# Moving the loads of two x tiles from SyncE's queue to ScalarE's at the start of a linear-attention block

## The chip, the cores and the metric

The kernel runs on one core of one Trainium2 chip. The metric is the device time of one execution in microseconds (us), smaller is better; the median of several runs counts. A profile is one further execution, recorded by the hardware profiler.

## What is computed

A block over one sequence of 2048 tokens with width 640: a layer norm without weights, then two branches from the normalized x, multiplied and added to the input.

```python
xn = (x - mean) / sqrt(var + 1e-5)                 # x: [2048, 640]
q, k, v = split_heads(xn @ wqkv)                   # 32 heads of 20
pq, pk = phi(q), phi(k)                            # t + 1 for t > 0, else exp(t); + 1e-6
kv = einsum("hsd,hse->hde", pk, v);  z = pk.sum(s)
s = ((pq @ kv) / (pq @ z + 1e-6)) @ wo             # linear attention, not causal
g = silu(relu(xn @ w1) @ w2)                       # w1: [640, 1728], w2: [1728, 640]
out = x + s * g
```

Inputs, weights and output are bfloat16.

## The kernel before

The tokens are 16 tiles of 128 (`T`), four tiles to a chunk of 512 columns. The work has a head, in which the first tiles are normalized, and a long body in which TensorE multiplies with few gaps.

**Normalizing.** Tiles 0 to 3 go a short way. ScalarE takes the sum of a tile (`ma`, L685, `mean_act`), or of its second half where VectorE's `bn_stats` (`ba`, `mh`, L637 and L679) takes the first. VectorE subtracts the mean (`ce`, L695 and L699, `centre`), TensorE transposes the centred tile with an identity matrix (`tr`, L706) and VectorE (`cd`) or ScalarE (`ca`) copies the transposed tile out of PSUM (L716, L718). Tiles 4 to 7 have `bn_stats` for mean and variance (`S`). All tiles are then normalized by VectorE (`N`, L673, `LN_norm`; it overwrites the centred tile, so it waits until TensorE has read that), and each `N` ends with a DMA transpose on SyncE's queue (L722, `xnT_dma`), which writes the transposed tile that the body multiplies with. The first eight of these transposes are those of tiles 0 to 7, in the order 1, 4, 5, 7, 6, 0, 2, 3.

**Key products.** `k012` is the part of tile 0's key product that uses weight rows 128 to 255 (row blocks 1 to 2); it multiplies on TensorE at L733 (`K_mm`) and needs the centred, transposed tile and the key weights. The key weights come in three loads (L586, `wk_load`): `lk02` with row blocks 0 and 1 (320 KB), `lk24` with 2 and 3 (320 KB), and `lk45` with block 4.

**Body.** Large products are done by a seven-product scheme of the Strassen kind (`unit`): products at L1164 accumulate in PSUM, and VectorE forms the sums of weight blocks, the sums of activations, and some additions from PSUM to PSUM, all through one helper (`tt`, L936). `SQ` forms the sums of the query weights, `wq`, a part of `reg6`; its first sum is written to a part of `pqT`. The query weights come by one load of 800 KB, `lq` (L567).

**Loads.** `lx3` loads x tile 3 on SyncE's queue and `ax1` loads x tile 1 on ScalarE's (L562, `x_load`, 160 KB a tile); `lx8` is a pair of tiles. `lw` loads a piece of w1 (L582).

**What sets the order.** The text `PROGRAM` lists all steps in order. A step becomes one or several recorded operations with the engine, the tiles it reads and writes, and so its dependencies. A planner (`Sched.place`, with the costs of `cost` and of `_record`) simulates the engines with estimated durations. TensorE and SyncE take their operations in the order of the text; in the head (up to the bar `|`) so do all other engines. After the bar ScalarE, VectorE and GpSimd take, among the next 60 recorded operations (`LOOK`), the one that is ready first by the planner's estimate, or a more urgent one. `emit` then writes each engine's instructions in that planned order with waits on semaphores. On the chip the order is fixed: an instruction that waits holds up all that follow it on its engine.

Of the kernel before, what the change touches and what calls it, by code (L numbers as in the profile page):

```python
# [343 lines left out]


PROGRAM = """
lx0 lx2 ax1 ba0 mh0 ma0 lk02 lx3 lk24 ce0 lx4 ma1 ce1 lx5 lk45 lx7 lw2 tr0 pf3 cd0 lx6 bb0 ma2 sq1
ce2 cd1 ma3 tr1 k001 lw5 cd2 k012 ba3 lw3 ca3 mh3 ag0 ce3 S4 tr2 k102 S5 ca4 k023 k123 k134 ca5 k201
lw0 N1 tr3 N4 sq2 k213 S7 ca6 k035 ca7 k145 N5 ke0 k235 S6 bb3 N7 ag3 k301 k312 kr0 ke1 kr1 F1
N6 k325 ke2 P4 N0 kr2 P11 P5 F0 ke3 P10 KT5 kr3 KT4 N2 N3 |  # L350
# [1631 lines left out]
```

## Time and profile before

| | |
|---|---|
| median of 3 runs | 202.5 us (201.94 to 203.0) |
| profiled execution: its own time | 202.56 us |
| its span (first to last instruction) | 201.3 us |
| granted TensorE clock | 1.00 |
| busy share of the span: TensorE, VectorE, ScalarE, GpSimd | 98%, 86%, 66%, 19% |
| DMA | 30.43 MB, mean 151 GB/s |

In the rows of the timeline the columns are start and duration in us, the engine, the line of the kernel, the operation, and output and input by tile name with buffer numbers left out (`reg<-reg` can be two different tiles). In brackets stands how long the engine was idle before and what released it. `SPq` and `ACTq` are the DMA issues of SyncE and ScalarE; "DMA to landing" counts from the issue to the last increment of the DMA's semaphore. `x4` is a count of instructions merged into one row. A wait for several semaphores is put down to the one that came last by the profile; where the named engine was long done, another, often a DMA, was the last.

### The profile page before, as it was taken

The page shows a single profiled execution, that of the slowest core. Times are in us where ns is not written, and L with a number is a line of the kernel's source. Part 1 is how long each engine was busy: PE and PEld are TensorE (multiplying, and loading weights), DVE is VectorE, ACT ScalarE, POOL GpSimd, SP SyncE. Part 2 cuts the span into 40 slices and gives each one's busy share as a digit, 9 for nine tenths or more (in the row PEclk, how much of TensorE's full clock was granted, in tenths as well). Part 3 has the DMA queues.
Part 4 walks back from the last instruction along what each step waited for, and adds up shares of the span by engine and source line. Part 5 has one row for each costly group of instructions (what it writes and reads, how often), then busy time and mean ns, then how long its engine had stood idle before and what let it go on. Part 6 is the DMA issues. An engine that isn't in the chain of part 4 may idle for free.

```text
span 201.3 us, 3641 instructions
## 1 busy us (share of the span) xinstructions
PE 197.2 (98%) x1312; PEld 120.1 (60%) x1312; DVE 173.2 (86%) x407; ACT 132.5 (66%) x280; POOL 37.7 (19%) x66
## 2 busy tenths in 40 slices
PE   8899999999999999999999999999999999999995
PEld 2656534554564554545454777777777777777773
DVE  5998799999999989999568998999867699866565
ACT  6798958998999998868832514363545355536533
POOL 3584003143345646422000000000000000000000
PEclk9999999999999999999999999999999999999999
DMA  5999695345466798854304985975952711011113
GB/s 179 335 259 95 150 351 144 70 98 109 108 145 134 150 256 174 171 99 67 113 17 118 270 264 184 295 212 148 355 185 72 258 65 36 33 67 65 36 65 98
DMA packets 38455, 30.43 MB, mean 151 GB/s; under 512 B 13733, under 2 KB 38437, under 8 KB 38437
## 3 DMA queue, kind: packets, MB, share of 16 engines
q1 hardware_dynamic: 32853, 23.62, 41.8%
q0 software_dynamic: 4624, 5.57, 14.3%
q10 hardware_dynamic: 960, 1.02, 1.7%
q8 instruction: 10, 0.16, 0.4%
q14 instruction: 8, 0.07, 0.1%
HBM read 15.81 MB, written 5.24 MB: 105 GB/s over the span
## 4 chain that ended last, share of the span: by engine, by line
PE 90%; DVE 4%; DMA 2%; ACT 1%; issue 1%; DVEq 0%
PE psT L991 43%; PE psT L1164 32%; PE psT L733 6%; PE psT L1494 2%; PE psT L823 2%; DMA reg<-reg 1%; ACT regE L743 1%; PE psT L1838 1%; DMA reg<-in_A_x_dram 1%; PE psT L841 1%; PE psT L1629 1%; PE psT L1603 1%; DVE stats L637 1%; DVE regX L936 1%; PE psT L895 1%
## 5 line engine op out<-in xcount | busy, mean ns | idle before, releaser
L1164 PE MATMUL psT<-reg 128*128 128x512 bf16 (+2 forms) x166 | 45.0, 370 | 0.0
L991 PE MATMUL psT<-reg,regH 128*128 128x320 bf16 (+1 forms) x224 | 35.0, 299 | 0.0
L991 PE MATMUL psT<-reg 128*128 128x320 bf16 (+1 forms) x178 | 28.4, 299 | 0.0
L991 PEld LDWEIGHTS psT<-reg,regH 128*128 128x128 bf16 (+1 forms) x224 | 21.9, 98 | 8.5
L1164 PEld LDWEIGHTS psT<-reg 128*128 128x128 bf16 (+1 forms) x166 | 15.9, 98 | 16.9 <-DVE regH L1217 0.6
L863 POOL DMA_DIRECT2D regH<-reg x16 | 18.6, 1188 | 20.9 <-DMA regH<-reg 9.4
L991 PEld LDWEIGHTS psT<-reg 128*128 128x128 f16 (+1 forms) x178 | 17.3, 98 | 7.4 <-DVE regE L899 0.4
L936 DVE TENSOR_TENSOR reg<-reg 128x1024 f16<-128x1024 bf16 (+11 forms) x30 | 19.0, 646 | 2.2 <-PE psT L991 1.8
L998 ACT ACTIVATE reg<-psT 128x320 f32<-128x320 f32 (+1 forms) x24 | 10.5, 436 | 15.8 <-PE psT L991 14.8
L1214 ACT ACTIVATE regH<-psT 128x512 bf16<-128x512 f32 (+1 forms) x24 | 14.6, 612 | 5.8 <-PE psT L1164 5.3
L1665 ACT ACTIVATE wv_sb<-psT 128x320 bf16<-128x320 f32 (+2 forms) x23 | 9.6, 424 | 11.4 <-PE psT L991 11.0
L991 PE MATMUL psT<-reg,pqT 128*128 128x320 bf16 (+1 forms) x84 | 15.8, 299 | 0.0
L936 DVE TENSOR_TENSOR psT<-psT,reg 128x320 f32<-128x320 f32 (+1 forms) x21 | 11.4, 543 | 2.8 <-PE psT L991 2.8
L637 DVE BATCH_NORM_STATS2 stats<-reg 128x6 f32<-128x320 bf16 x28 | 12.3, 480 | 1.4 <-DMA reg<-in_A_x_dram 1.1
L1853 ACT ACTIVATE reg<-psT 128x640 bf16<-128x640 f32 (+1 forms) x14 | 8.0, 570 | 7.5 <-PE psT L991 7.5
L733 PE MATMUL psT<-reg 128*128 128x320 bf16 x80 | 12.3, 299 | 0.0
L936 DVE TENSOR_TENSOR reg<-psT,reg 128x320 bf16<-128x320 f32 (+1 forms) x16 | 7.8, 489 | 5.1 <-PE psT L991 5.1
L1171 ACT ACTIVATE psT<-psT 128x512 f32<-128x512 f32 (+1 forms) x18 | 10.6, 594 | 1.8 <-PE psT L1164 1.7
L800 ACT ACTIVATE regE<-psT 128x512 bf16<-128x512 f32 x16 | 9.5, 603 | 2.6 <-PE psT L1164 2.5
L998 ACT ACTIVATE psT<-psT 128x320 f32<-128x320 f32 x17 | 7.2, 425 | 5.6 <-PE psT L991 5.5
L936 DVE TENSOR_TENSOR reg<-reg,wv_sb 128x640 bf16<-128x640 bf16 (+1 forms) x15 | 6.8, 456 | 4.3 <-ACT reg L1853 3.5
L733 PEld LDWEIGHTS psT<-reg 128*128 128x128 bf16 x80 | 7.7, 98 | 4.5 <-issue 0.4
(174 smaller groups left out, 400.0 us busy)
## 6 DMA issues: line engine op xcount, KB each, us to landing
regH<-reg POOLq DMA_DIRECT2D x16, 320.0 KB, 3.8
reg<-in_B_w_dram SPq DMA_DIRECT2D x12, 320.0 KB, 4.9
scr<-rden SPq DMA_DIRECT2D x4, 640.0 KB, 7.0
reg<-in_A_x_dram SPq DMA_DIRECT2D x4, 640.0 KB, 6.1
out_dram<-reg SPq DMA_DIRECT2D x14, 160.0 KB, 1.8
regE<-scr SPq DMA_DIRECT2D x3, 640.0 KB, 6.1
reg<-in_A_x_dram SPq DMA_DIRECT2D x4, 320.0 KB, 4.8
reg<-in_A_x_dram SPq DMA_DIRECT2D x7, 160.0 KB, 4.3
```

The lines of the kernel that those rows point to most:

```text
L637: sc.op("DVE", lambda eng: eng.bn_stats(stats[:, t, a, :], xv[:, HN * a:HN * (a + 1)]), R=[("xin", xs(t))], W=[("stats", t, a)])
L733: fns.append(lambda eng, a=a, k=k, lhs=lhs: eng.matmul(ps[bk[a]][:, 0:HN], lhsT=lhs, rhs=wk[:, k, HN * a:HN * (a + 1)], start=(k == 0), st ...
L800: exps.append(sc.op("ACT", lambda eng: eng.activation(out=e_, in_=src, func=ACTF.Exp), R=[key], W=[("er_e", es)]))
L863: dma("POOL", lambda eng: eng.dma_start(zacc[a], src, **kw), R=[key] + after, W=[("zacc", a)], chain=zchain[a])
L936: sc.op("DVE", lambda eng: eng.tensor_tensor(out=out, in0=in0, in1=in1, op=op), R=R, W=W, extra=extra)
L991: sc.group("PE", [(lambda eng, k=k, lhs=lhs, rhs=rhs: eng.matmul(ps[b][:, 0:HN], lhsT=lhs, rhs=rhs, start=(start and k == 0), stop=(k == n ...
L998: sc.op("ACT", lambda eng: eng.activation(out=dst, in_=ps[b][:, 0:HN], func=ACTF.Copy), R=[("ps", b)], W=[dkey], extra=extra)
L1164: sc.group("PE", [(lambda eng, k=k, lhs=lhs, rhs=rhs: eng.matmul(ps[b][:, 0:nn], lhsT=lhs if tile is None else rhs, rhs=rhs if tile is Non ...
L1171: sc.op("ACT", lambda eng: eng.activation(out=dst[:, 0:nn], in_=ps[b][:, 0:nn], func=ACTF.Copy), R=[("ps", b)], W=[dkey], extra=extra)
L1214: sc.op("ACT", lambda eng: eng.activation(out=dst, in_=ps[b], func=ACTF.Relu), R=[("ps", b)], W=[("hT", j, f)], extra=ex)
L1665: sc.op("ACT", lambda eng, lo=lo, hi=hi: eng.activation(out=g[:, lo:hi], in_=src[:, lo - HN * n:hi - HN * n], func=ACTF.Silu), R=[key, ("s ...
L1853: sc.op("ACT", lambda eng: eng.activation(out=o_[:, 0:n].rearrange("p (a n) -> p a n", a=2) if n == D else o_[:, 0:n], in_=src, func=ACTF. ...
```

## The change

One line of `PROGRAM` changes. The loads of x tiles 2 and 3 leave SyncE's queue (`lx2`, `lx3`) and stand behind that of x tile 1 on ScalarE's (`ax2`, `ax3`). SyncE's queue then begins with x tile 0, `lk02`, `lk24` and goes on with x tile 4 as before.

```diff
 PROGRAM = """
-lx0 lx2 ax1 ba0 mh0 ma0 lk02 lx3 lk24 ce0 lx4 ma1 ce1 lx5 lk45 lx7 lw2 tr0 pf3 cd0 lx6 bb0 ma2 sq1
+lx0 ax1 ax2 ax3 ba0 mh0 ma0 lk02 lk24 ce0 lx4 ma1 ce1 lx5 lk45 lx7 lw2 tr0 pf3 cd0 lx6 bb0 ma2 sq1
 ce2 cd1 ma3 tr1 k001 lw5 cd2 k012 ba3 lw3 ca3 mh3 ag0 ce3 S4 tr2 k102 S5 ca4 k023 k123 k134 ca5 k201
```

Both names call the same function; the second only names another engine as issuer:

```python
        "lx": x_load,
        "ax": lambda t: x_load(t, 1, "ACT"),
```

Since the planner simulates the whole kernel, other operations can move in its order too.

## The prediction, made before the result was known

> **What bounds the kernel now.** I read the page's busy table first, then TensorE's own rows and the chain of waits, and last the rows of SyncE, VectorE and ScalarE up to 30 us.
>
> ```profile
> span 201.3 us, 3641 instructions
> PE 197.2 (98%) x1312; PEld 120.1 (60%) x1312; DVE 173.2 (86%) x407; ACT 132.5 (66%) x280; POOL 37.7 (19%) x66
> ```
>
> TensorE is busy for 197.2 of 201.3 us. A change at the start can only pay by closing an idle stretch of TensorE, and only if no later stretch opens by as much. The timeline of TensorE has two places where that is decided:
>
> ```profile
> 6.04 0.70 PE L733 MATMUL psT<-reg,regX 128*128 128x320 bf16 x4 [0.63 <-DVE regX L716]
> ...
> 27.17 1.24 PE L823 MATMUL psT<-reg 128*128 128x512 bf16 x5
> 28.58 0.60 PE L1164 MATMUL psT<-regX,reg 128*128 128x512 f16 x2 [0.17 <-DVE psT L936]
> ```
>
> The first key product starts at 6.04 after 0.63 us of idleness. The row names a copy, but the product also waits for the first key weights (`lk02`). Their own row and its time to landing:
>
> ```profile
> L586 SPq DMA_DIRECT2D reg<-in_A_wqkv_dram x1: 434/434/434, 1.7 to 1.7; - x1
> DMA to landing us min/median/max: 4.2/4.2/4.2
> ```
>
> Issued at 1.7, landed at 5.9: this DMA, not the copy, releases the product. The change goes for these 0.63 us.
>
> The second place is the product at 28.58. The chain of waits does not reach it through TensorE but through transposes and VectorE:
>
> ```profile
> 21.05 2.64 DMA reg<-reg
> ...
> 23.72 0.43 DVE regH L936
> ...
> 27.93 0.61 DVE psT L936
> 28.54 0.05 issue
> 28.58 9.24 PE psT L1164 x42
> ```
>
> From 28.58 on, all the rest of the chain up to the last tile is TensorE back to back. So the end of the kernel moves with 28.58, and 6.04 matters only if it moves 28.58.
>
> What leads there starts on SyncE's queue:
>
> ```profile
> 10.17 12.16 SPq L722 DMA_TRANSPOSE reg<-reg  x8
> ...
> 23.00 0.46 SPq L567 DMA_DIRECT2D reg<-in_A_wqkv_dram  x1
> ...
> 17.07 2.61 SPq L722 DMA_TRANSPOSE reg<-reg  x1
> ...
> 21.05 1.28 SPq L722 DMA_TRANSPOSE reg<-reg  x1
> ```
>
> Eight transposes issue back to back from 10.17 to 22.33 (a usual one 1.28 us, one of them 2.61), the last lands at 21.05 + 2.64 = 23.69, and VectorE starts at 23.72. So 28.58 hangs on when the first transpose issues, and that needs the normalized tile 1 from VectorE (L673, 9.74 to 10.14).
>
> **The change part by part.**
>
> **1. Key weights 0.45 us earlier.** On SyncE `lk02` takes the slot of x tile 2, the second of two issues:
>
> ```profile
> 0.79 0.88 SPq L562 DMA_DIRECT2D reg<-in_A_x_dram  x2
> ...
> L562 SPq DMA_DIRECT2D reg<-in_A_x_dram x2: 399/408/417, 0.8 to 1.3; - x2
> DMA to landing us min/median/max: 2.3/2.5/2.7
> ...
> 0.96 0.39 ACTq L562 DMA_DIRECT2D reg<-in_A_x_dram  x1
> ...
> DMA to landing us min/median/max: 2.6/2.6/2.6
> ```
>
> The two end at 0.79 + 0.88 = 1.67 and the second takes 0.42, so `lk02` is issued at 1.25 instead of 1.7. If it keeps its 4.2 us it lands at 5.45 and the first key product starts up to 0.45 us earlier; if the x tiles on the other queue take their share of the DMA engines it lands as late as before. Either way I cost this at nothing: what hides it is the wait at 28.58, where TensorE would idle that much longer. Were that cover gone, it would be worth 0.45 us at most.
>
> **2. x tiles 2 and 3 on ScalarE's queue.** Before, by the rows just shown, x tile 2 lands at 1.25 + 2.7 = 3.95 and x tile 1 (ScalarE's queue, the last two rows) at 0.96 + 2.6 = 3.56. After, x tile 2 is issued behind x tile 1, at some 0.96 + 0.39 + 0.05 = 1.40, and moves beside `lk02`, not ahead of it. ScalarE's own work isn't held up: its third issue is over by about 2.3, and its first mean needs x tile 0, which lands at 0.79 + 2.3 = 3.1.
>
> ```profile
> core 0: us, PE busy (x) PEld busy (x) DVE busy (x) ACT busy (x) POOL busy (x), PEclk, DMA share, GB/s
> 2.20:3.30 1.10, 1.10 (x4) 0.32 (x3) 0.15 (x1) 0.24 (x2) 0.34 (x1) 1.00 1.00 341
> 3.40:4.40 1.00, 0.86 (x4) 0.16 (x3) 0.93 (x4) 1.00 (x5) 0.00 (x0) 1.00 0.81 223
> ```
>
> The engines are full (share 1.00, 341 GB/s) up to 3.3; then, when the key weights begin, they slow down to 223 GB/s. If x tile 2 shares evenly with `lk02`, 2 x 160 KB must move after x tile 1: 0.96 us at 341 GB/s, 1.47 us at 223. So x tile 2 lands at 4.5 to 5.0. I take 4.75; the ends are 4.0 (no sharing: 1.40 + 2.6) and 5.9 (1.40 plus the 4.5 us of x tile 4, below). The Trainium skill (DMA: Bandwidth & Descriptors, Issuing engines are not separate DMA queues) says that DMAs of several issuing engines interleave on the same 16 DMA engines and that a second queue saves only issue time. By that rule the sum is the one I take below; without sharing it would be that of rival (b).
>
> Who waits for x tile 2? ScalarE's mean, then VectorE's centring, then everything behind it on VectorE in its fixed order:
>
> ```profile
> 4.34 0.72 ACT L685 ACTIVATE regE<-reg 128x640 bf16<-128x640 bf16 x1
> ...
> 6.33 0.47 ACT L685 ACTIVATE regE<-reg 128x320 bf16<-128x320 bf16 x1 [0.46 <-DMA reg<-in_A_x_dram]
> ...
> 5.38 0.37 DVE L695 TENSOR_SCALAR reg<-reg,msum 128x640 bf16<-128x640 bf16 x1
> 5.67 0.55 DVE L716 COPY regX<-psT 128x384 bf16<-128x384 bf16 x2
> 6.34 0.49 DVE L637 BATCH_NORM_STATS2 stats<-reg 128x6 f32<-128x320 bf16 x1
> ...
> 7.12 0.45 DVE L699 TENSOR_SCALAR reg<-reg,msum 128x640 bf16<-128x640 bf16 x1
> 7.70 0.89 DVE L637 BATCH_NORM_STATS2 stats<-reg 128x6 f32<-128x320 bf16 x2
> ...
> 9.74 0.40 DVE L673 TENSOR_SCALAR reg<-reg,msum,rsy 128x640 bf16<-128x640 bf16 x1
> ```
>
> The mean moves from 4.34 to 4.78, 0.44 later, and the centring at 5.38 with it. Two gaps on VectorE take some of it back: 6.22 to 6.34 (waiting for x tile 3, which now comes earlier) and 7.57 to 7.70 (x tile 4, issued at 3.2 and landed 4.5 later, at 7.7):
>
> ```profile
> L562 SPq DMA_DIRECT2D reg<-in_A_x_dram x1: 467/467/467, 3.2 to 3.2; - x1
> DMA to landing us min/median/max: 4.5/4.5/4.5
> ```
>
> x tile 4 has the same bytes ahead of it as before, so it lands no later than 7.7 and does not bind. Tile 1's normalization, and with it the first transpose, comes 0.44 - 0.12 - 0.13 = 0.19, say 0.2 us later. Ends: 0.25 earlier (both gaps closed, x tile 2 in time) and 1.3 later (x tile 2 at 5.9: 1.55 - 0.25).
>
> **3. The planner's new order on VectorE.** The built program differs in one more place. TensorE's order is the same, but on VectorE, by line:
>
> ```
> before: L761, L637, L936 psT<-psT, L936 regX, L936 pqT<-reg6, L637, L936 pqT
> after:  L761, L936 pqT<-reg6, L936 psT<-psT, L936 regX, L936 pqT, L637, L637
> ```
>
> `pqT<-reg6` (first sum of `SQ`) reads the query weights, the load `lq` that SyncE issues behind all eight transposes and `lx8`. It now stands ahead of the addition into PSUM on which TensorE waits at 28.58.
>
> ```profile
> 27.04 0.48 DVE L761 TENSOR_TENSOR reg<-regE 128x640 bf16<-128x640 bf16 x1
> 27.44 0.49 DVE L637 BATCH_NORM_STATS2 stats<-reg 128x6 f32<-128x320 bf16 x1
> 27.84 0.68 DVE L936 TENSOR_TENSOR psT<-psT,wv_sb 128x512 f32<-128x512 f32 x1
> ...
> 28.76 0.42 DVE L936 TENSOR_TENSOR pqT<-reg 128x512 f16<-128x512 bf16 x1
> 29.10 0.49 DVE L637 BATCH_NORM_STATS2 stats<-reg 128x6 f32<-128x320 bf16 x1
> ...
> reg<-in_A_wqkv_dram SPq DMA_DIRECT2D x1, 800.0 KB, 5.3
> ```
>
> `lq` lands at 23.00 + 5.3 = 28.3. VectorE would be ready for the sum at 27.44, waits 0.86 us, spends 0.34 on it (28.76 to 29.10) and starts the addition at 28.66 instead of 27.84: 0.82 us later. Queued behind the waiting instruction are that addition and all later VectorE work; TensorE waits for the addition. Transposes, VectorE's chain and `lq` all shift with the first transpose, so 0.82 and the 0.2 of part 2 add up. Ends: a gain of 0.06 if `lq` is there in time (0.34 in the place of the 0.40 of L637), and 0.82.
>
> **Sum.** 0 + 0.2 + 0.82 = 1.0 us later at 28.58, with nothing idle behind it to absorb it. The profiled execution took 202.56 us, its span 201.3 and 1.26 around it; the median of the runs is 202.5, so they stand alike: 202.56 + 1.0 = 203.6.
>
> **The rivals.** (a) The forecast: wait for `lq`, and x tile 2 somewhat late: 203.1 to 204.0. (b) x tile 2 comes by 4.4, so the head is no later or up to 0.25 earlier, and only the wait for `lq` is paid: +0.57 to +0.82, 203.1 to 203.4. For it: ScalarE's queue got x tile 1 in 2.6 us beside x tile 0. (c) The key weights' slow stretch holds up x tile 2 in full, landing at 5.3 to 5.9: the head 0.7 to 1.3 later, +1.5 to +2.1, some 204.3. For it: 223 GB/s with the same weights. (d) Not slower: `lq` is there before VectorE reaches the sum. It decides at 27.44, that is if `lq` takes under 4.4 us in place of 5.3; with the head 0.25 earlier the product starts at 28.27 and the time is 202.2. Against it: `lq` has 800 KB and `lx8` 320 KB ahead of it, which at 341 GB/s take 3.3 us after the last transpose at 23.69, 27.0 without any latency. (e) The one transpose of 2.61 us takes 1.28 like its neighbours: the whole chain 1.33 earlier, +1.0 - 1.33, 202.2; nothing in the change does this on purpose. (f) The change does not do what it says, `lk02` lands no earlier: by part 1 the time is that of (a) to (c).
>
> **How the numbers follow.** (a) 0.50, (b) 0.12, (c) 0.24, (d) 0.07, (e) 0.07; (f) lies within them. A measurement of this kernel can tell about 0.5% from no change, 1.0 us, so the line runs at 203.5, within (a): 0.30 of it lies above, 0.20 below. Slower: 0.30 + 0.24 = 0.54. Within: 0.20 + 0.12 + 0.07 + 0.07 = 0.46, of which I give 0.04 to faster, for (d) and (e) together: the product at 28.58 can't start before TensorE is through the rows ahead of it (27.17 + 1.24 = 28.41, less 0.45 if the key products start earlier), so 0.62 us is the most that can be won, but the three runs spread from 201.94 to 203.0. So 0.42 within. The range leaves out most of (d), (e) and the end of (c): 202.6 to 204.4.
>
> **What would show it.** In the trace after: `lk02` issued near 1.25; the mean of x tile 2 on ScalarE starting near 4.8 with a DMA named as releaser; the first transpose at about 10.4; on VectorE an idle stretch of about 0.86 us before `pqT<-reg`, ended by a DMA of in_A_wqkv; TensorE's L1164 at about 29.6 with over 1 us of idleness. If TensorE starts that product at 28.6 or earlier, the forecast is wrong: in part 3 if VectorE shows no wait, in part 2 if the transposes start before 10.17.

## The result and the profile after

| | before | after |
|---|---|---|
| median | 202.53 us (4 runs, 201.94 to 203.0) | 204.45 us (4 runs, 204.27 to 204.68) |
| after / before | | 1.0094, 95% interval 1.0065 to 1.0122 |
| profiled execution: its own time | 202.56 us | 204.53 us |
| its span | 201.3 us | 203.0 us |

The change costs 1.9 us, nearly twice the 1.0 us of the forecast, and just outside the range given. The direction and both mechanisms of the forecast are in the trace. Of the 1.97 us between the two profiled executions, 1.7 lie in the span and 0.27 around it.

The page's first lines show a TensorE that does the same work in a longer span: 0.9 us more busy, 0.8 us more idle.

```profile
span 203.0 us, 3641 instructions
PE 198.1 (98%) x1312; PEld 121.0 (60%) x1312; DVE 172.6 (85%) x407; ACT 132.5 (65%) x280; POOL 37.5 (18%) x66
```

TensorE's timeline of after, at the two places that the prediction named:

```profile
5.95 1.10 PE L733 MATMUL psT<-reg,regX 128*128 128x320 bf16 x4
...
30.27 0.61 PE L1164 MATMUL psT<-regX,reg 128*128 128x512 f16 x2 [1.35 <-DVE psT L936]
```

The first key product is 0.09 us earlier and no longer waits. The product that followed the addition at 28.58 now starts at 30.27, 1.69 us later, after 1.35 us of idleness: that is the lengthening of the span (1.7). The chain of waits of after shows where it comes from:

```profile
1.87 5.49 DMA reg<-in_A_x_dram
...
22.67 0.58 SPq L562
23.30 5.85 DMA reg<-in_A_wqkv_dram
29.52 0.70 DVE psT L936
30.27 9.24 PE psT L1164 x42
```

It goes through two DMAs: x tile 3, issued at 1.87 on ScalarE's queue, and `lq`, issued at 23.30. In the chain of before the stretch up to the addition was closed by the last transpose and VectorE, and `lq` did not stand in it.

Here are the head's rows in the timelines of SyncE, ScalarE and VectorE of after, then those of VectorE around 28 us:

```profile
0.96 1.36 ACTq L562 DMA_DIRECT2D reg<-in_A_x_dram  x3
1.25 0.93 SPq L586 DMA_DIRECT2D reg<-in_A_wqkv_dram  x2
...
5.19 0.74 ACT L685 ACTIVATE regE<-reg 128x640 bf16<-128x640 bf16 x1 [0.59 <-DMA reg<-in_A_x_dram]
...
6.05 0.39 DVE L695 TENSOR_SCALAR reg<-reg,msum 128x640 bf16<-128x640 bf16 x1 [0.42 <-ACT regE L685]
7.38 0.49 DVE L637 BATCH_NORM_STATS2 stats<-reg 128x6 f32<-128x320 bf16 x1 [0.48 <-DMA reg<-in_A_x_dram]
10.56 0.40 DVE L673 TENSOR_SCALAR reg<-reg,msum,rsy 128x640 bf16<-128x640 bf16 x1
10.99 11.63 SPq L722 DMA_TRANSPOSE reg<-reg  x8
```

```profile
27.33 0.49 DVE L761 TENSOR_TENSOR reg<-regE 128x640 bf16<-128x640 bf16 x1
29.17 0.43 DVE L936 TENSOR_TENSOR pqT<-reg 128x512 f16<-128x512 bf16 x1 [1.35 <-DMA reg<-in_A_wqkv_dram]
29.52 0.69 DVE L936 TENSOR_TENSOR psT<-psT,wv_sb 128x512 f32<-128x512 f32 x1
```

`lk02` is issued at 1.25, as forecast. x tile 2 holds up ScalarE until 5.19 and VectorE until 6.05, and then x tile 3 holds up VectorE until 7.38, where before it came at 6.34. Tile 1 is normalized at 10.56 (before 9.74) and the first transpose issues at 10.99 (before 10.17). By the rows of SyncE's queue the eight transposes end at 10.99 + 11.63 = 22.62 us (before at 10.17 + 12.16 = 22.33), and VectorE's row before the sum starts at 27.33 (before at 27.04): of the 0.82 us by which the first transpose is late, 0.29 arrives there. Near 28 us VectorE stands 1.35 us in front of `pqT<-reg`, the first sum of `SQ`, while the addition that TensorE needs stands behind it. So in this profile most of the 1.69 us comes from the wait for `lq`.

The landing times of after, from the answers for the lines of the key weights and of the x loads (1.3 to 2.0 us; three issues on ScalarE's queue):

```profile
L586 SPq DMA_DIRECT2D reg<-in_A_wqkv_dram x2: 421/445/469, 1.3 to 1.7; - x2
DMA to landing us min/median/max: 3.5/4.7/5.9
...
L562 ACTq DMA_DIRECT2D reg<-in_A_x_dram x3: 401/445/453, 1.0 to 1.9; - x3
DMA to landing us min/median/max: 2.7/3.8/5.5
```

`lk02` lands at 1.25 + 3.5 = 4.8 in place of 5.9, x tile 2 at 1.4 + 3.8 = 5.2 in place of 3.95, x tile 3 at 1.87 + 5.5 = 7.36 in place of 6.3.

### The profile page after: what moved, and what is told of

Its sections match the earlier page's. It is cut to its first block, busy times and chain, and to the rows that moved or that the text cites. A ratio compares the mean times of both kernels' runs of the same rounds, so it can differ in the third digit from the quotient of the medians.

```text
span 203.0 us, 3641 instructions
## 1 busy us (share of the span) xinstructions
PE 198.1 (98%) x1312; PEld 121.0 (60%) x1312; DVE 172.6 (85%) x407; ACT 132.5 (65%) x280; POOL 37.5 (18%) x66
## 3 DMA queue, kind: packets, MB, share of 16 engines
q10 hardware_dynamic: 1248, 1.34, 2.2%
## 4 chain that ended last, share of the span: by engine, by line
PE 89%; DMA 6%; ACT 2%; DVE 1%; issue 1%; SPq 0%; ACTq 0%; DVEq 0%
PE psT L991 42%; PE psT L1164 32%; PE psT L733 5%; DMA reg<-in_A_wqkv_dram 3%; DMA reg<-in_A_x_dram 3%; PE psT L1494 2%; PE psT L823 2%; ACT regE L743 1%; PE psT L1838 1%; PE psT L841 1%; PE psT L1629 1%; PE psT L1603 1%; PE psT L895 1%; DVE psT L936 0%; DVE reg L936 0%
## 5 line engine op out<-in xcount | busy, mean ns | idle before, releaser
L637 DVE BATCH_NORM_STATS2 stats<-reg 128x6 f32<-128x320 bf16 x28 | 12.3, 481 | 1.8 <-DMA reg<-in_A_x_dram 1.8
```

What stands on the lines that cost most here:

```text
L637: sc.op("DVE", lambda eng: eng.bn_stats(stats[:, t, a, :], xv[:, HN * a:HN * (a + 1)]), R=[("xin", xs(t))], W=[("stats", t, a)])
```

## The experiments

**Theory A**: two causes add, the late x tiles in the head and the new order on VectorE, each worth more than the forecast gave it. **Theory B**: the late x tiles do it all, and the order only decides where the wait is seen. A third cause was found on the way.

The planner's order can be set apart from the loads by one number: told that `lq` lands 0.6 us later or earlier, it places the first sum of `SQ` behind or ahead of the addition, and all else stays.

### The loads without the order, the order without the loads

The loads of after, in VectorE's order of before:

```diff
-lx0 lx2 ax1 ba0 mh0 ma0 lk02 lx3 lk24 ce0 lx4 ...
+lx0 ax1 ax2 ax3 ba0 mh0 ma0 lk02 lk24 ce0 lx4 ...
-            lag = 0.5 if names[1] == "scr" ... else 0.0
+            lag = 0.5 if names[1] == "scr" ... else 0.0 if size != 819200 or names[1] != "in_A_wqkv_dram" else 0.6
```

> The loads as after the change, but VectorE's order as before it (the planner is told that the query weights land 0.6 us later, which puts their first sum behind the addition again). Theory A (two causes add up: the sum that waits for the query weights, and x tiles 2 and 3 landing late): the wait before the addition is gone, the addition starts about 28.1 (27.84 plus the 0.30 us by which the transposes end later after the change), TensorE's product at 28.9, the time 202.8. Theory B (the late x tiles alone made the loss, the wait merely fills time that would be lost anyway): the product stays near 30 and the time is 204 or more.

The loads of before, in VectorE's order of after: line 161 alone, with -0.6 in the place of 0.6.

> The loads as before the change, but VectorE's order as after it (the planner is told that the query weights land 0.6 us earlier). Theory A: the sum waits from 27.4 until the query weights land at about 28.3, the product at 28.58 starts at about 29.4, the time is 0.8 us longer, 203.4. Theory B: the time stays at 202.5.

| | median | ratio to before | median span (before 201.4) |
|---|---|---|---|
| loads alone | 203.44 us | 1.0027 (1.0005 to 1.0049) | 201.85 us |
| order alone | 203.99 us | 1.0049 (1.0022 to 1.0075) | 202.75 us |

VectorE and TensorE in the loads alone, then in the order alone:

```profile
28.41 0.68 DVE L936 TENSOR_TENSOR psT<-psT,wv_sb 128x512 f32<-128x512 f32 x1
...
29.15 0.60 PE L1164 MATMUL psT<-regX,reg 128*128 128x512 f16 x2 [0.17 <-DVE psT L936]
```

```profile
28.99 0.43 DVE L936 TENSOR_TENSOR pqT<-reg 128x512 f16<-128x512 bf16 x1 [1.28 <-DMA reg<-in_A_wqkv_dram]
29.33 0.69 DVE L936 TENSOR_TENSOR psT<-psT,wv_sb 128x512 f32<-128x512 f32 x1
...
30.09 0.60 PE L1164 MATMUL psT<-regX,reg 128*128 128x512 f16 x2 [1.23 <-DVE psT L936]
```

With the loads alone VectorE doesn't wait near 28 us and the product is 0.57 us late, all of it from the head. With the order alone the loads at the start are those of before and VectorE waits 1.28 us for `lq`. Both runs are slower than expected (202.8 and 203.4). In spans the first costs 0.45 us and the second 1.35, together 1.8; the span of after is 1.6 us longer in its own runs and 2.15 in the repetition below. The sizes are rough: the ratios are worth 0.55 and 0.99 us, while the medians lie 0.76 and 1.31 us above that of before beside them (202.68). Theory B falls: the order costs without any late x tile.

What is late in the head of the loads alone, on ScalarE and on TensorE:

```profile
5.75 0.74 ACT L685 ACTIVATE regE<-reg 128x640 bf16<-128x640 bf16 x1 [1.28 <-DMA reg<-in_A_x_dram]
...
7.20 0.45 ACT L685 ACTIVATE regE<-reg 128x320 bf16<-128x320 bf16 x1
```

```profile
5.70 0.70 PE L733 MATMUL psT<-reg,regX 128*128 128x320 bf16 x4 [0.24 <-DMA reg<-in_A_wqkv_dram]
...
7.05 0.61 PE L706 MATMUL psT<-ident,reg 128*128 128x128 bf16 x5 [0.65 <-DVE reg L695]
```

x tile 2 holds ScalarE up for 1.28 us; x tile 3 holds up nobody here, unlike in after. The first key product starts 0.34 us earlier than before (5.70 for 6.04), and then TensorE stands 0.65 us until tile 2 is centred. So TensorE loses the earlier start again to the late x tile.

### One tile at a time

x tile 2 alone on ScalarE's queue, then x tile 3 alone, both in VectorE's order of before (the planner's numbers for `lq`, and for x loads on ScalarE's queue in the second, raised by 0.6 us):

```diff
+lx0 ax1 ax2 ba0 mh0 ma0 lk02 lx3 lk24 ce0 lx4 ...
```

> Only x tile 2 goes to ScalarE's queue; x tile 3 stays on SyncE's behind the first key weights; VectorE's order as before the change. Theory A1 (the two queues are served transfer by transfer in turn: x0, x1, first key weights, x2, x3, second key weights): x tile 2 lands at about 5.2 as after the change, x tile 3 at 5.5 to 6.3, so the second VectorE gap is as before and the normalized tile 1 comes 0.2 to 0.5 later than before; the time is 202.5 to 202.9. Theory A2 (ScalarE's queue gets an even share): x tile 2 at 4.5 to 5.0, tile 1 normalized at most 0.2 later, time 202.5.

```diff
+lx0 lx2 ax1 ax3 ba0 mh0 ma0 lk02 lk24 ce0 lx4 ...
```

> Only x tile 3 goes to ScalarE's queue, behind x tile 1; x tile 2 stays second on SyncE's, the first key weights third; VectorE's order as before the change. Theory A1 (transfer by transfer in turn: x0, x1, x2, x3, first key weights): x tile 3 lands at about 4.5 to 5.0 instead of 6.3, the gap before its statistics closes, tile 1 is normalized 0.1 to 0.25 earlier; the key weights land up to 0.4 later, which the wait at 28.58 hides; time 202.2 to 202.5. Theory A2 (even share): x tile 3 lands at 5.0 to 6.0, time 202.4 to 202.5. If ScalarE's queue simply comes last, x tile 3 lands after 6.5 and the time is over 202.8.

x tile 2 alone: 202.78 us, ratio 1.0011 (0.9994 to 1.0027), the span no longer than before's (201.4). Its mean on ScalarE is as late as in after:

```profile
5.39 0.74 ACT L685 ACTIVATE regE<-reg 128x640 bf16<-128x640 bf16 x1 [0.82 <-DMA reg<-in_A_x_dram]
...
6.84 0.45 ACT L685 ACTIVATE regE<-reg 128x320 bf16<-128x320 bf16 x1
```

x tile 2 lands at 1.4 + 4.0 = 5.4 and x tile 3, still on SyncE's queue, at 1.7 + 4.1 = 5.8, as Theory A1 expected. x tile 3 is there when ScalarE comes to it at 6.84 (no wait): most of the delay of x tile 2 falls into the gap that before had in front of x tile 3. By the spans the head costs nothing with x tile 2 alone and 0.45 us with both tiles. What the second tile adds stays open: in four of the five profiles with the loads of after x tile 3 is in time as here, and in those four and in this one the first transpose issues 5.2 us after x tile 2's mean starts, at 5.32 to 6.10 there and at 5.39 here.

x tile 3 alone: 203.19 us, 1.0021 (0.999 to 1.0052); the time is unclear, and not the 202.2 to 202.5 of Theory A1. TensorE, then VectorE in this run:

```profile
7.00 0.70 PE L733 MATMUL psT<-reg,regX 128*128 128x320 bf16 x4 [0.99 <-DVE mv L641]
...
29.05 0.61 PE L1164 MATMUL psT<-regX,reg 128*128 128x512 f16 x2
```

```profile
8.14 0.89 DVE L637 BATCH_NORM_STATS2 stats<-reg 128x6 f32<-128x320 bf16 x2 [0.76 <-DMA reg<-in_A_x_dram]
...
28.31 0.68 DVE L936 TENSOR_TENSOR psT<-psT,wv_sb 128x512 f32<-128x512 f32 x1
```

x tile 3 lands early, at 1.4 + 3.7 = 5.1, but the first key weights land at 1.7 + 5.2 = 6.9 in place of 5.9, and the first key product starts at 7.00. The row names VectorE; the copy that the product needs was done by 6.25, so the weights were the last. x tile 4 is late too (8.14 for 7.70), and the addition ends at 28.99. The product starts at 29.05, 0.47 us later than before, with no wait named: TensorE's path from the key products and VectorE's path through the addition are late alike.

### `lq` ahead of `lx8`

If VectorE waits for `lq`, an earlier `lq` must take part of it back. The text's `lx8 lq` becomes `lq lx8`, in after and in before; in before, too, the planner then gives VectorE the order of after.

```diff
-SH0_1 F2 lx8 lq SH0_2 ...
+SH0_1 F2 lq lx8 SH0_2 ...
```

> The kernel after the change with one more swap: the query weights are issued ahead of the x pair 8 and 9 instead of behind it. VectorE's order stays that of after. Theory A (the sum that waits for the query weights is one of two causes): they land some 0.95 us earlier (320 KB less ahead of them), near 27.2 to 28.2 instead of 29.15, so the wait of 1.35 us before the sum shrinks to under 0.5; the time falls by 0.7 to 1.3, to 203.2 to 203.8. Theory B (only the late x tiles): it stays at 204.2 or more.

> The loads of before, with the query weights issued ahead of the x pair 8 and 9. The planner then puts the first sum of the query weights ahead of the addition, as in the kernel after. Theory A: with the weights there in time the early sum costs little; TensorE's product starts between 28.5 and 28.9, the time is 202.5 to 203.0, about 1 us below the run with old loads and new order. If the early sum is bad by itself, not by its wait, the time is 203.5 or more.

After with it: 203.84 us, 1.0059 (1.0035 to 1.0084). Before with it: 202.91 us, 1.0014 (0.9998 to 1.003). VectorE in the two, in this order:

```profile
28.44 0.42 DVE L936 TENSOR_TENSOR pqT<-reg 128x512 f16<-128x512 bf16 x1 [0.42 <-DMA reg<-in_A_wqkv_dram]
```

```profile
28.13 0.43 DVE L936 TENSOR_TENSOR pqT<-reg 128x512 f16<-128x512 bf16 x1 [0.77 <-DMA reg<-in_A_wqkv_dram]
```

After waits 0.42 us in place of 1.22 (after again, run beside it) and takes 203.84 in place of 205.01 us. Before in the new order takes 0.36 us more than in the old one, not 1.3 as with `lx8` first; its profile still has a wait of 0.77 us, so `lq` was not there in time even so. So it is the wait for `lq` that the new order costs; the head's share stays.

### Both kernels once more

> The kernel before, unchanged, for a second profile of it. If the first profile was a typical one, the first transpose issues at 10.2, the query weights land 5.3 us after their issue and the product starts at 28.6. If it was a lucky one: first transpose 10.6 to 10.9, query weights 5.8 to 6.1 after their issue, product at 28.6 to 29.0.

> The kernel after, unchanged, timed beside the others on the same chip. Theory A (the parts add up): the loads alone measured 0.27% and the order alone 0.49%, so 0.76%, 204.2. If the two help each other on, 204.6 or more; if they overlap, under 203.9.

Before again: 202.72 us, one run; the runs of before beside it had a median of 202.55 (21 runs). After again: 205.01 us, 1.0113 (1.0082 to 1.0145). That is in the branch in which the two parts help each other on (204.6 or more); the 204.45 of the result is not. x tile 2 lands at 1.4 + 4.7 = 6.1 here and at 5.2 there. Whether the parts only add stays open. The answer for `lq`'s line and VectorE's row in before again, and VectorE's row in after again:

```profile
DMA to landing us min/median/max: 6.0/6.0/6.0
...
29.12 0.43 DVE L936 TENSOR_TENSOR pqT<-reg 128x512 f16<-128x512 bf16 x1 [0.23 <-DMA reg<-in_A_wqkv_dram]
```

```profile
29.60 0.42 DVE L936 TENSOR_TENSOR pqT<-reg 128x512 f16<-128x512 bf16 x1 [1.22 <-DMA reg<-in_A_wqkv_dram]
```

In this execution of the same kernel `lq` took 6.0 us, not 5.3, and even the old order waits for it, behind the addition where it costs nothing. The 5.3 us on which the forecast rested was the short end: the twelve profiles with `lx8` ahead of `lq` have 5.0 to 6.1. The first transpose issues at 10.59: by the expectation, the first profile was a lucky one. TensorE in before again:

```profile
6.54 0.70 PE L733 MATMUL psT<-reg,regX 128*128 128x320 bf16 x4 [0.83 <-DVE regX L716]
...
28.63 0.60 PE L1164 MATMUL psT<-regX,reg 128*128 128x512 f16 x2
```

```profile
27.89 0.68 DVE L936 TENSOR_TENSOR psT<-psT,wv_sb 128x512 f32<-128x512 f32 x1
```

The addition ends at 28.57 and the product starts at 28.63, 22.09 us after the first key product; no wait is named in front of it. How early TensorE could be there by itself show three runs below, in which the addition is first and x tiles 2 and 3 are on SyncE's queue: there the addition is over 0.19 to 0.26 us ahead of the product, and the product starts 21.99 or 22.00 us after the first key product. So in before again TensorE's path from the key products and VectorE's path through the addition end within 0.1 us of each other. Earlier key weights win nothing here while the addition comes last, and later ones would cost their delay less those 0.1 us.

### The addition first

If the place of the addition decides, it should pay to put it ahead of what stands before it in the old order, the `bn_stats` of L637 (0.40 us). On the loads of before, and on those of after (there with the planner's number for `lq` raised by 0.6 us, so that the rest of VectorE's order is that of before):

```diff
-        return sorted(recs, key=lambda o: (o.start, o.n))
+        dve = sorted((o for o in recs if o.E == "DVE"), key=lambda o: (o.start, o.n)); dve[65].start = dve[64].start - 1e-4; return sorted(...)
```

> The kernel before with one swap on VectorE: the addition into PSUM stands ahead of the statistics of x tile 8, so it starts 0.40 us earlier (27.44 instead of 27.84). Theory A (the addition sets the product at 28.58): the product starts at 28.2 to 28.3, 0.3 us earlier, then TensorE itself is the bound; time 202.2 to 202.5. If the product waits for something else, it stays at 28.6 and 202.6.

> The loads of after, the query weights' sum behind the addition as before, and the addition also ahead of the statistics of x tile 8. Here the first key product starts early (5.6 to 5.9). Theory A (head 0.5 later, addition 0.4 earlier): the product at 28.6 to 28.8, time 202.6 to 202.9. If the earlier key weights pay once VectorE no longer holds the product, the time is below that of the run with before's loads and the same swap.

On the loads of before: 202.25 us, 0.9985 (0.9971 to 0.9999), the lowest median of all here and just clear of 1. On those of after: 203.19 us, 1.0034 (1.0018 to 1.0049), above the 202.6 to 202.9 expected. VectorE and TensorE of the former:

```profile
27.20 0.70 DVE L936 TENSOR_TENSOR psT<-psT,wv_sb 128x512 f32<-128x512 f32 x1
...
28.16 0.59 PE L1164 MATMUL psT<-regX,reg 128*128 128x512 f16 x2
```

TensorE does not wait for the addition here. With TensorE's own rows as the bound, earlier key weights could have paid, and they don't: with the same order, the loads of after are 0.94 us slower, 0.65 us of it in the span. In the two profiles the first key product starts 0.20 us earlier with the loads of after (5.96 for 6.16) and the product near 28 us 0.19 us later (28.35 for 28.16).

### What lies around the span

With every execution's time stands its span. The difference of the two, over all kernels so far:

| x loads that ScalarE issues at the start | kernels | time less span, mean of each kernel |
|---|---|---|
| one (tile 1) | before; order alone; `lq` first on before; addition first on before | 1.23 to 1.26 us |
| two | tile 2 alone; tile 3 alone | 1.39, 1.40 us |
| three | after, and the four others with its loads | 1.56 to 1.58 us |

Single executions lie within 0.1 us of these. So the moved loads cost 0.16 us each before or behind the span, where no row of a profile shows it: 0.32 us in after. Is it a price of every DMA that ScalarE issues? Two kernels, both with the addition first and the loads of before, move DMAs off ScalarE: the two loads of the value weights (at 107 and 118 us), then x tile 1 as well. The main line of the first (a further line records each load's source; the second kernel's condition takes every load of an input):

```diff
-        seq = self.place()
+        seq = self.place(); [setattr(o, "E", "SP") for o in seq if o.kind == "dma" and o.E == "ACT" and o.src == "in_A_wqkv_dram"]
```

> The kernel before with the addition first (the run before), and the two loads of the value weights (480 and 320 KB, issued at 107 and 118 us) on SyncE's queue at the same planned place; nothing else moves. The time of a run less its span is 1.23 to 1.26 us for every kernel so far that has the loads of before, 1.39 with one x tile moved to ScalarE's queue, 1.57 with both. Theory N, each DMA on ScalarE's queue costs 0.16 us outside the span wherever it stands: 1.25 - 2 x 0.16 = 0.93, and about 202.25 - 0.3 = 201.95 in all if SyncE isn't held up. Theory H, only loads in the head do it: 1.25 and 202.25. Theory B, it goes with bytes (0.32 us for 320 KB): 1.25 - 0.8 = 0.45, 201.45.

> As the run before, and x tile 1 on SyncE's queue too, so that ScalarE issues no load, only the last store. Theory N: 0.77 us outside the span; theory H: 1.09; theory B: 0.29. Inside the span x tile 2 and the key weights are issued some 0.45 us later; the first key product has cover up to the addition, x tile 2 has some 0.3 us of it, so the span grows by 0 to 0.45. The total by N: 201.8 to 202.25.

Both keep 1.25 us: theories N and B fall, late loads don't count; and H falls as it was put, since without x tile 1 it is 1.25 too. The times are 202.46 us (0.9984, 0.9966 to 1.0003) and 202.45 us (0.9986, 0.997 to 1.0002), no gain over the addition first alone. So of the loads at ScalarE's start the first is free and the second and third cost 0.16 us each. All of them were x tiles of 160 KB, so number and bytes at the start are not told apart. Why, and whether it lies ahead of the span or behind it, stays open.

## Why the prediction was wrong

**What held.** TensorE bounds the kernel, and the end moves with the product after the addition: 1.69 us there, 1.7 us in the span, and in all fourteen profiles the span ends 172.7 to 173.0 us after that product starts. Part 1 held in its conclusion: the key weights came 1.1 us earlier in this profile, more than the 0.45 allowed, and bought nothing. Its reason, that the addition sets the product, holds in before again as well, though by under 0.1 us there. In the loads alone the earlier start was also used up before that, by TensorE's wait for tile 2 (0.65 us). Both other parts cost in the way described: x tile 2 holds up ScalarE's mean, and VectorE waits for `lq` in front of the addition. Of the rivals, (b) and (d) did not happen. (c), x tile 2 held up in full, came nearest with some 204.3 us, and x tile 2 did land at 5.2 to 6.1; but it missed the longer wait and what lies outside the span, and it asked 0.7 to 1.3 us of a head that cost 0.45, so the nearness of its number is in part luck. Rival (e) did not happen either: one transpose of the eight is the slow one in after too (2.34 us in place of 2.61).

**What failed**, by the terms of the sum (spans of many executions):

| term | forecast | measured |
|---|---|---|
| key weights earlier | 0 | not measured by itself, contained in the next row |
| x tiles 2 and 3, head | 0.2 us | 0.45 us (loads alone) |
| order on VectorE, wait for `lq` | 0.82 us | 1.35 us (order alone) |
| around the span | not in the sum | 0.32 us |
| sum | 1.0 us | 2.1 us, against 1.9 and 2.5 for the two measurements of after; 1.5 by the ratios |

*The third part's size* came from one issue of `lq`, 5.3 us to landing. In after it took 5.85, in the order alone 5.8, in after again 5.7: 0.86 + 0.5 = 1.36 us of wait, against 1.22 to 1.35 in these three. The 0.82 was set down as the upper end, though the row could not bound the landing time from above.

*The second part's size* came from an even split of the DMA engines between the two queues, by which x tile 2 would land at 4.75. It lands at 5.2 in after and at 5.3 to 6.1 in the four other profiles with its loads. Five profiles with the loads of after have the first transpose at 10.54 to 11.32 us, mean 10.97; six with those of before at 10.17 to 10.88, mean 10.46. The one profile that the forecast had was the earliest of the six.

*The second part's step "waiting for x tile 3, which now comes earlier"* was wrong too. x tile 3 is issued 0.3 us earlier and lands later: at 7.36 for 6.3 in the first two profiles, at 7.0 to 7.4 for 6.3 to 7.0 in all profiles with the loads of after and of before. It now moves beside `lk24`, and the last section shows how uneven that can be. In after the gap in front of it therefore didn't give 0.12 us back but grew to 0.48. In the four other profiles with these loads x tile 2 was the later one, and x tile 3 held up nobody.

*"All shift with the first transpose"* held only roughly: VectorE near 27 us is 0.29 us late in after where the first transpose is 0.82 late, and 0.57 (27.61) where it is 0.80 late in the loads alone, because the eight transposes took 12.16 us in the profile of before, the longest of the eleven with either set of loads, and 11.63 and 11.92 in these two. The early first transpose and the long train of that one profile nearly cancel.

*The sum itself* was made on the span, and took what lies around it (1.26 us) as a constant. It isn't one here.

The range's upper end, 204.4, left out only a part of rival (c); with `lq` at up to 6.1 us it would have reached 0.8 us higher.

## What to carry to other kernels

Moving a load to another queue is no gain in itself: ask what the planner does with the new estimate, and look for an instruction on the critical engine that now waits for a DMA ahead of the operation the bound needs; one such swap cost three times what the late loads cost in the span. Where two paths end within 0.1 us of each other, delaying either one costs. A DMA's landing time read off one profile is a sample, so put its spread over several issues into the range, and as a term of both signs. Make the sum against the time and not only against the span: what lies outside can change too.

## What the runs showed of the hardware

**Two queues don't share evenly over a microsecond.** The DMA queues of after in three windows, 3 to 4, 4 to 5 and 6 to 7 us (packets, MB, share of 16 engines; q1 is SyncE's, q10 ScalarE's), and q10 over the whole run on its page:

```profile
q1 hardware_dynamic: 229, 0.29, 87.0%
q10 hardware_dynamic: 48, 0.04, 12.5%
...
q1 hardware_dynamic: 157, 0.19, 56.9%
q10 hardware_dynamic: 146, 0.17, 48.0%
...
q1 hardware_dynamic: 284, 0.33, 91.8%
q10 hardware_dynamic: 44, 0.04, 13.6%
...
q10 hardware_dynamic: 1248, 1.34, 2.2%
```

Two x tiles are 288 packets (before's page has 960 in place of 1248), so one is 144, 9 for each of the 16 engines. Up to 3 us ScalarE's queue had moved 101, so if it is served in order, 43 of the 48 packets of the first window are the rest of x tile 1, and x tile 2, issued at 1.4, had got next to nothing by 4 us while SyncE's queue moved 229. Then x tile 2 got nearly half; then, with x tile 3 still unfinished, ScalarE's queue got 44 of 328. The four other profiles with these loads show the same swing (28 to 40, 111 to 148 and 33 to 42 packets in these windows). The forecast's even split put x tile 2 at 4.75 us; the five profiles have its mean start at 5.19 to 6.10. The Trainium skill (DMA: Bandwidth & Descriptors, Queues, rings and completion order) says that an engine takes a whole packet of some 9 to 17 descriptors from one queue before it turns to the next; if the trace's packets are those descriptors, a tile is one turn, which agrees with the swings. No run here shows the turns of a single engine. The rule that the prediction used, that a second queue brings no DMA engines of its own, agrees with these windows, in which the two queues' shares add up to 99.5, 104.9 and 105.4% of the 16 engines; the even sharing that I made of it did not hold.

**Loads of x tiles at ScalarE's start cost time outside the span**, 0.16 us for each beyond the first, by the table above.

**One issue of the eight DMA transposes is slow in every profile**, 2.34 us in after and 2.61 in before, 2.34 to 2.89 over all fourteen, where a usual one takes 1.28. Its cause stays open.
